# Four batches of value-head sums, gate products on VectorE, and an exchanged pair of loads in a fused attention-plus-MLP block

## The chip, the cores and the metric

One core of one Trainium2 chip. The time is the device time of one execution in microseconds (us). Most executions of one kernel agree within about 0.3%. All runs told here are with a granted clock of 0.999 or 1.0.

Engines in the profile: PE is TensorE's matmuls, PEld its weight loads, DVE is VectorE, ACT ScalarE, POOL GpSimd, SP SyncE. `L1374` is line 1374 of the kernel that ran; the changed kernel's lines are moved against those of before (its L723 is L720 of before, L1374 is L1335, L1220 is L1204, L1274 is L1253; with the bank edit of the experiments L1374 becomes L1376).

## The reference, cut to what matters

```python
# S = 2048 tokens, D = 640, H = 32 heads of 20, window W = 8 with dilation 2, F = 1536; bf16
xn = layernorm(x)
q, k, v = split(xn @ wqkv)                       # [H, S, 20] each
kg, vg = k[s - 2*w], v[s - 2*w]                  # w = 0..7, masked where s - 2*w < 0
attn = softmax(sum_d(q * kg) * scale)            # [H, S, 8]
o = sum_w(attn * vg)                             # the "value head sums"
h = (xn @ w_gate) * (xn @ w_up)                  # the gate product, no activation
out = x + o @ wo + h @ w_down
```

## The kernel before

A small scheduler inside the kernel orders the work of all engines at build time: each piece is a `Task` on an engine, and the scheduler orders instructions from its own estimate of when each will end.

The loads at the start. All but one small transfer (`touch`, by ScalarE) go out through SyncE, one after the other; `x_load` is a tile of 128 tokens (160 KB), `wqkv_load(0, 0, 3)` the first three fifths of the Q columns (480 KB), here "the Q rows".

```python
x_load(0, land=3.2)
...
wqkv_load(0, 0, 3, land=5.3)
x_load(1, land=5.7)
wqkv_load(0, 3, NCH, land=7.0)
```

The value sums. VectorE multiplies probabilities with values (`PV`), GpSimd adds pairs (`SV`), and TensorE sums over the window with a 128x32 selector. A unit is one chunk of one block of 512 tokens, 20 units in all. `BATCH` names the last unit of each batch of sums on TensorE, and each unit takes one bank.

```python
NU = NJ * NCH
BATCH = (1, 4, 6, 9, 11, 14, 19)
...
for u, b in zip(us, bs):
    for dq in range(4):
        ... e.matmul(PS[32*dq:32*dq+32, b, :], SEL[:], SV[sv_of[u]][:, dq, :], ...)
```

The gate product: gate and up projection of 128 features each fill a bank; ScalarE copies gate to SBUF, then either VectorE multiplies it with the up bank, or ScalarE copies that too and GpSimd multiplies.

```python
def mul():
    X = op("dve", lambda e: e.tensor_tensor(h, h, PS[:, hold[1], :], ALU.mult), ...)
    K.free_bank(hold[1], X)
...
if on_pool(j, m):
    ...  # ScalarE copies the up bank into us, GpSimd multiplies h by us
```

The choice of a bank: of the free banks, the one that is free earliest by the scheduler's estimate.

```python
def choose(self, k, free):
    if not k.contig:
        return [b for _, b in free[:k.banks]]
...
def free_bank(self, b, X):
    self.banks[b] = X.end + 0.05
```

Of the kernel before, what the change touches and what calls it, by code (L numbers as in the profile page):

```python
# [6 lines left out]
ALU = mybir.AluOpType  # L7
# [3 lines left out]
D = 640  # L11
# [4 lines left out]
NF = 12  # L16
# [5 lines left out]
TS = 128  # L22
JB = 512
# [332 lines left out]
def build_kernel(nc, A_x, A_wqkv, A_wo, B_x, B_w_gate, B_w_up, B_w_down, out):  # L356
# [41 lines left out]
    SV += [sb("SV3", [128, 4, JB], at=a_qk + 33024), sb("SV4", [128, 4, JB], at=a_qk + 33024 + 4096)]  # L398
    SV += [sb("SV5", [128, 4, JB], at=a_ra + 6 * D * 2)]
    sv_free = [3, 4, 0, 1, 2]  # L400
    a_sc = place[0]
# [10 lines left out]
    LOG = [sb(f"LOG{i}", [128, 2, W, TS]) for i in range(2)]  # L412
    HX = [sb(f"HX{i}", [128, JB], at=place[0] - 8192 + i * 1024) for i in range(8)]
    PRD += [sb("PRD9", [128, 4, JB], at=place[0])]
    HX += [sb(f"HX{8 + i}", [128, JB]) for i in range(4)]
    ATX0 = sb("ATX0", [128, 2, 2, JB])
# [13 lines left out]
    NUX = 3  # L430
    UX = sb("UX", [128, NUX, JB])
    STATS = sb("STATS", [128, NT, 12], FP32)
    MV = sb("MV", [128, NT, 2], FP32)
    SD = sb("SD", [128, NT, 4], FP32)
    DUM = sb("DUM", [128, 16], FP32)
    TCH = sb("TCH", [128, NCH, 32])
    ZERO = sb("ZERO", [128, JB])
    EPSC = sb("EPSC", [128, 16], FP32)
    IDENT = sb("IDENT", [128, 128])
# [5 lines left out]
    def ht(j, m):  # L445
        if j == 3:
            return XNT[:, m % NCH, m // NCH * JB:(m // NCH + 1) * JB]
        if j == 2:
            return OT[:, 3, m - 8, :] if m >= 8 else HX[HXM[m]][:]
        return HT[:, j, m, :]  # L450

    HXM = (0, 1, 2, 3, 8, 9, 10, 11, 4, 5, 6, 7)
    WPOS = (2, 0, 1)
# [6 lines left out]
    def bump(*k):  # L460
        count[k] = count.get(k, 0) + 1
# [45 lines left out]
    def wqkv_load(g, lo=0, hi=NCH, eng="sp", land=None):  # L507
        dst = WQKV[:, WPOS[g], lo:hi, :]
        dma(dst, wqkv_src[:, lo:hi, g * D:(g + 1) * D], w=[dst], name=f"ld_wqkv{g}_{lo}", eng=eng, land=land)
# [324 lines left out]
    def products():  # L834
        rows = {j: [] for j in range(NJ)}
        holds = {}
        for at, (j, kind) in enumerate(ORDER):
# [10 lines left out]
            if len(rows[j]) == 10 - 3 * len(QUAD.get(j, ())):  # L848
                K.spawn(logits(j, rows[j]))
        mark("products")  # L850
# [109 lines left out]

    def logits(j, slots):
        hold = []
        for e in slots:
            if len(e) > 3:
                yield lambda: len(e[3]) == 2
        slots.sort(key=lambda e: -e[2])
        n1 = sum(e[2] for e in slots)

        def go(*bs):
            for i, e in enumerate(slots):  # L970
                n, s, r = e[:3]
                b, i, nt = bs[1 - r], i - (0 if r else n1), n1 if r else len(slots) - n1
                for a in range(4):
                    o = PS[32 * a:32 * a + 32, b, :].rearrange("p (q s) -> p q s", q=4)
                    x = s[:, :, a * TS:(a + 1) * TS]
                    op("pe", (lambda o, x, i, a, nt: lambda e: e.matmul(o, G[:], x, start=(i == 0), stop=(i == nt - 1),  # L976
                                                                   tile_position=(0, 32 * a)))(o, x, i, a, nt),
                       r=[G[:], x], w=[o], name=f"lg{j}_{r}_{i}_{a}", occ=0.054, lat=0.4, mode=1)
                free.append(n)
            hold.extend(bs)  # L980

        def dst(r):
            return LOG[j // 2][:, j % 2, 4 * r:4 * r + 4, :]

        def ev(r):
            b, d = hold[1 - r], dst(r)
            X = op("act", lambda e: e.activation(d, PS[:, b, :].rearrange("p (q s) -> p q s", q=4), ACT.Copy, scale=SCALE),  # L987
# [8 lines left out]

        yield Task("pe", go, r=[e[1][:] for e in slots], prio=9.5, banks=2, slack=2.0 if j in QUAD else 0.5)
        bump("lg")
        for r in (1, 0):
            yield Task("act", lambda: ev(r), r=[PS[:, hold[1 - r], :]], w=[dst(r)], prio=2)  # L1000
        bump("logits", j // 2)

# [62 lines left out]
    NU = NJ * NCH  # L1065
    BATCH = (1, 4, 6, 9, 11, 14, 19)

# [43 lines left out]
    def unit(u):  # L1111
# [3 lines left out]
        yield have("vx", u)  # L1115
        if not more and count.get(("dn", 0), 0) >= 8:
            more.append(1)
            sv_free.extend(range(NS, len(SV)))
        yield lambda: len(sv_free) > 0 and (sv_free[0] in (3, 4) or count.get(("lg",), 0) >= NJ)
# [100 lines left out]

    ucount = [0]

    def on_pool(j, m):
        return count.get(("lg",), 0) >= NJ and m < 11 and ucount[0] - count.get(("hp",), 0) < HP_MAX

    def gu(j):
# [14 lines left out]
        for m in range(NF):  # L1241
# [15 lines left out]
            def after(h=h, hold=hold, j=j, m=m):  # L1257
# [11 lines left out]
                if on_pool(j, m):  # L1269
# [18 lines left out]
                    return  # L1288
                yield Task("dve", mul, r=[h, PS[:, hold[1], :]], prio=H_PRIO)

# [28 lines left out]
    def dn_piece(j, t, nb, rows, c0, c1):  # L1319
# [64 lines left out]
        K.spawn(tail())  # L1384

    SLIP = 0.3
    N_PE_T = 4
# [6 lines left out]
    GU_KEEP = 3  # L1394
    HP_MAX = 2
    ORDER = ((0, "n"), (1, "n"), (2, "n"), (3, "n"), (2, "w"), (3, "w"))
    LAST = ORDER[-1][0]
    HP_PRIO = 30
    DN_KEEP = 3
    H_PRIO = 9  # L1400
# [4 lines left out]
    stores.append(dma(TCH[0:16], tch, w=[TCH[0:16]], name="touch", eng="act"))  # L1405
    wqkv_load(0, 0, 3, land=5.3)
    x_load(1, land=5.7)
    wqkv_load(0, 3, NCH, land=7.0)
# [70 lines left out]
```

## Time and profile before

| | before |
|---|---|
| time, 3 runs | 267.78 us median (267.72 to 267.81) |
| span of the profiled execution | 266.0 us |
| TensorE busy | 98% |
| batches of value sums on TensorE | 7 |
| first 25 projection matmuls start | 6.39 us |
| row of 50 projection matmuls starts | 8.69 us |
| from there to the last addition on VectorE | 254.98 us |

The last line leaves out the first 9 us (loads from memory) and the last 2.3 us (stores to memory). I call it "the body".

### The profile page before, as it was taken

Reading aid. Unit: us, or ns where it says so; the run is one execution under the profiler, and the core shown is the slowest. Engines: PE = TensorE matmul, PEld = TensorE weight load, DVE = VectorE, ACT = ScalarE, POOL = GpSimd, SP = SyncE. Lnnn points to the kernel's source line nnn. Section 1 sums busy time; section 2 is a strip of 40 time slices with the busy share of each in tenths; the row PEclk is TensorE's granted clock in tenths of the full one; section 3 lists DMA queues with packets and bytes.
Section 4 is the critical chain, followed back from the end, with each engine's and each line's share of the span. In section 5 each row is a group of like instructions: output and inputs, shape, how many; then the busy total and the mean of one; then the engine's idle time right before and its main releaser. Section 6 shows DMA issues by size and latency. Waiting matters only on the chain.

```text
span 266.0 us, 4403 instructions
## 1 busy us (share of the span) xinstructions
PE 260.7 (98%) x1747; PEld 151.8 (57%) x1764; DVE 217.0 (82%) x249; ACT 112.0 (42%) x203; POOL 154.5 (58%) x99
## 2 busy tenths in 40 slices
PE   8999999999999999999999999999999999999996
PEld 5996965444444444444444444667466746774775
DVE  4687899999998699898699998998699979961211
ACT  3469997556622212242365426432443243116100
POOL 3000000000644996299955599999999989999000
DMA  7963689960489993831399143553885385006101
GB/s 211 372 208 78 126 149 382 385 248 1 124 147 192 241 212 75 166 76 30 73 334 201 36 112 83 133 147 80 182 181 157 85 146 112 2 0 94 32 25 53
DMA packets 39685, 37.84 MB, mean 142 GB/s; under 512 B 15824, under 2 KB 37328, under 8 KB 39632
## 3 DMA queue, kind: packets, MB, share of 16 engines
q1 hardware_dynamic: 36688, 31.35, 43.6%
q0 software_dynamic: 2736, 6.16, 13.6%
q8 instruction: 14, 0.23, 0.4%
q10 hardware_dynamic: 240, 0.05, 0.1%
q14 instruction: 7, 0.06, 0.1%
HBM read 25.07 MB, written 7.23 MB: 121 GB/s over the span
## 4 chain that ended last, share of the span: by engine, by line
PE 92%; ACT 5%; issue 1%; DVE 0%
PE PS L1253 39%; PE PS L1335 28%; PE PS L688 17%; ACT XNS L599 3%; PE PS L976 2%; PE PS L720 2%; PE PS L1204 2%; PE PS L672 2%; ACT QT L693 1%; ACT VST L693 1%; PE PS L632 1%; ACT KT L693 1%; ACT SD L574 0%; ACT HX L693 0%; DVE XNT L642 0%
## 5 line engine op out<-in xcount | busy, mean ns | idle before, releaser
L1154 POOL TENSOR_TENSOR SV<-PV 128x1024 bf16<-128x1024 f32 x40 | 95.0, 2535 | 9.6 <-DVE LOG L1033 3.3
L1149 DVE TENSOR_TENSOR PV<-VX,PS 128x1024 f32<-128x1024 bf16 (+1 forms) x54 | 91.0, 1729 | 5.4 <-POOL SV L1154 4.5
L688 PE MATMUL PS<-XNT,WQKV 128*128 128x512 bf16 (+2 forms) x384 | 60.0, 315 | 0.7 <-issue 0.5
L1253 PE MATMUL PS<-XNT,WG 128*128 128x512 bf16 x235 | 58.6, 379 | 0.3
L1253 PE MATMUL PS<-XNT,WU 128*128 128x512 bf16 x234 | 58.4, 379 | 0.4 <-ACT HX L693 0.2
L688 PEld LDWEIGHTS PS<-XNT,WQKV 128*128 128x128 bf16 x390 | 37.8, 112 | 22.1 <-ACT LOG L987 0.8
L1253 PEld LDWEIGHTS PS<-XNT,WU 128*128 128x128 bf16 x240 | 23.2, 98 | 29.0 <-issue 0.8
L1253 PEld LDWEIGHTS PS<-XNT,WG 128*128 128x128 bf16 x240 | 23.5, 98 | 27.8
L910 DVE TENSOR_TENSOR PRF<-PS,KT 128x1024 f32<-128x1024 f32 x32 | 37.8, 1216 | 0.3 <-PE PS L688 0.3
L693 ACT ACTIVATE HT<-PS 128x512 bf16<-128x512 f32 x24 | 14.3, 597 | 41.9 <-PE PS L1253 41.9
L936 POOL TENSOR_TENSOR PRF<-PRF,PRF 128x1024 f32<-128x1024 f32 x8 | 18.8, 2359 | 21.8 <-DVE LOG L1033 20.6
L1335 PE MATMUL PS<-WD,HT 128*128 128x320 bf16 x192 | 28.7, 299 | 0.0
L693 ACT ACTIVATE FB<-PS 128x320 bf16<-128x320 f32 x24 | 10.5, 438 | 41.1 <-PE PS L1335 38.4
L863 DVE TENSOR_TENSOR PRD<-QT,KT 128x2048 bf16<-128x2048 bf16 x24 | 27.3, 1217 | 0.0
L1335 PE MATMUL PS<-WO,OT 128*128 128x320 bf16 (+1 forms) x165 | 27.0, 295 | 0.0
L995 POOL MEMSET LOG<- 32x6 bf16 (+6 forms) x7 | 0.4, 95 | 44.2 <-ACT LOG L987 44.2
L1335 PEld LDWEIGHTS PS<-WD,HT 128*128 128x128 bf16 x192 | 18.6, 98 | 8.2 <-ACT FB L693 0.4
L1262 DVE TENSOR_TENSOR HT<-HT,PS 128x512 bf16<-128x512 bf16 x24 | 16.4, 685 | 8.0 <-PE PS L1253 7.9
L1335 PEld LDWEIGHTS PS<-WO,OT 128*128 128x128 bf16 x165 | 15.8, 98 | 6.2 <-issue 0.4
L954 POOL TENSOR_TENSOR PRD<-PRF,PRF 128x1024 bf16<-128x1024 f32 x8 | 18.7, 2354 | 0.9 <-DVE PRF L910 0.8
L1348 DVE TENSOR_TENSOR FB<-PS,XR 128x320 bf16<-128x320 f32 (+1 forms) x9 | 4.1, 454 | 15.3 <-PE PS L1335 15.3
L564 DVE BATCH_NORM_STATS2 STATS<-XST 128x6 f32<-128x320 bf16 x32 | 14.1, 471 | 2.4 <-DMA XST<-in_A_x_dram 2.4
(69 smaller groups left out, 238.9 us busy)
## 6 DMA issues: line engine op xcount, KB each, us to landing
VX<-v_scratch SPq DMA_DIRECT2D x80, 130.0 KB, 3.0
PRF<-PRF POOLq DMA_DIRECT2D x8, 512.0 KB, 5.2
XST<-in_A_x_dram SPq DMA_DIRECT2D x16, 160.0 KB, 5.6
v_scratch<-VST SPq DMA_DIRECT2D x4, 640.0 KB, 5.8
WG<-in_B_w_gate_dram SPq DMA_DIRECT2D x1, 1920.0 KB, 7.9
WU<-in_B_w_up_dram SPq DMA_DIRECT2D x1, 1920.0 KB, 11.9
out_dram<-in_A_x_dram SPq DMA_DIRECT2D x1, 1920.0 KB, 18.4
WD<-in_B_w_down_dram SPq DMA_DIRECT2D x1, 1920.0 KB, 8.5
```

The lines of the kernel that those rows point to most:

```text
L564: op("dve", lambda e: e.bn_stats(o, a), r=[a], w=[("st", t, i)], name=f"bn{t}_{i}", occ=0.49)
L688: op("pe", (lambda o, l, x, c, first: lambda e: e.matmul(o, l, x, start=first, stop=(c == NCH - 1)))(o, l, x, c, first), r=[l, x], w=[o], ...
L693: X = op("act", (lambda o, i: lambda e: e.activation(o, i, ACT.Copy))(o, i), r=[i], w=[o], name=name, occ=0.12 + n * 0.9e-3)
L863: op("dve", lambda e: e.tensor_tensor(s[:], qb, kv, ALU.mult), r=[q, rk], w=[s[:]], name=f"prod{j}_{r}_{c}", occ=1.15, lock=True)
L910: X = op("dve", lambda e: e.tensor_tensor(o[:], qb, kv, ALU.mult), r=[q, rk, ("qev", j, c)], w=[o[:]], name=f"prow{j}_{r}_{c}_{q0}", occ=1.17)
L936: yield Task("pool", lambda: op("pool", lambda e: e.tensor_tensor(x, x, y, ALU.add), r=[x, y] + tokens(), w=[x], name=name, occ=2.36, lock ...
L954: yield Task("pool", lambda: op("pool", lambda e: e.tensor_tensor(o, a, y, ALU.add), r=[a, y] + tokens(), w=[o], name=f"qend{j}_{r}_{q0}", ...
L1149: op("dve", lambda e: e.tensor_tensor(p, vw, a, ALU.mult), r=[vv] + rk, w=[p], name=f"pv{u}_{x}_{r0}", occ=0.09 + 1.1 * nr)
L1154: X = op("pool", lambda e: e.tensor_tensor(o, p[:, :, 0, :], p[:, :, 1, :], ALU.add), r=[p[:]] + tokens(), w=[o], name=f"pva{u}_{x}", occ= ...
L1253: op("pe", (lambda l, x, c: lambda e: e.matmul(PS[:, b, :], l, x, start=(c == 0), stop=(c == NCH - 1)))(l, x, c), r=[l, x], w=[PS[:, b, :] ...
L1262: X = op("dve", lambda e: e.tensor_tensor(h, h, PS[:, hold[1], :], ALU.mult), r=[h, PS[:, hold[1], :]], w=[h], name=f"h{m}_{j}", occ=0.65)
L1335: op("pe", (lambda l, x, i: lambda e: e.matmul(dst, l, x, start=(i == 0), stop=(i == n - 1)))(l, x, i), r=[l, x], w=[PS[:, b, :]], name=f" ...
```

## The change

The intent: three switches of TensorE between 128-wide and 32-wide matmuls fewer; gate products taken off GpSimd so that GpSimd's additions are ready for the larger batches; and the second token tile loaded ahead of the Q rows, so that VectorE need not wait for it. Cut to its core (more `SV` buffers, the three steps in which they come free, and a way to join logits that is switched off are left out):

```diff
-    BATCH = (1, 4, 6, 9, 11, 14, 19)
+    BATCH = (4, 9, 14, 19)
...
-                yield Task("dve", mul, r=[h, PS[:, hold[1], :]], prio=H_PRIO)
+                if not fast(j, m):
+                    yield Task("dve", mul, r=[h, PS[:, hold[1], :]], prio=H_PRIO)
+                    return
+                k0 = fcount[0]
+                fcount[0] += 1
+                us = UF[k0 % NUF][:]
+
+                def fev():
+                    K.free_bank(hold[1], evac([(us, PS[:, hold[1], :], JB)], f"uev{m}_{j}"))
+
+                def fmul():
+                    op("dve", lambda e: e.tensor_tensor(h, h, us, ALU.mult), r=[h, us], w=[h], name=f"h{m}_{j}", occ=0.34, lock=True)
...
+    FAST = [(2, m) for m in range(NF)]
...
-    HP_MAX = 2
+    HP_MAX = 0
...
-    DN_KEEP = 3
+    DN_KEEP = 5
...
-    wqkv_load(0, 0, 3, land=5.3)
-    x_load(1, land=5.7)
+    x_load(1, land=3.65)
+    wqkv_load(0, 0, 3, land=5.75)
```

`HP_MAX = 0` ends the gate products on GpSimd. `FAST` names those of the third block, whose up bank ScalarE copies to SBUF. The fourth block's are multiplied straight from PSUM by VectorE. `DN_KEEP` is how many free banks a piece of the down projection must leave: five, so that a batch of five finds its banks.

More of the change, by code (lines that the diff above doesn't have):

```diff
@@ L399, in build_kernel @@
     SV += [sb("SV5", [128, 4, JB], at=a_ra + 6 * D * 2)]
+    SV += [sb(f"SV{6 + i}", [128, 4, JB], at=a_ra + NF * JB * 2 + i * 4096) for i in range(3)]
     sv_free = [3, 4, 0, 1, 2]
@@ L412, in build_kernel @@
     LOG = [sb(f"LOG{i}", [128, 2, W, TS]) for i in range(2)]
-    HX = [sb(f"HX{i}", [128, JB], at=place[0] - 8192 + i * 1024) for i in range(8)]
+    HX = [sb(f"HX{i}", [128, JB], at=place[0] - 8192 + i * 1024) for i in range(4)]
+    SV += [sb("SV9", [128, 4, JB], at=place[0] - 4096)]
     PRD += [sb("PRD9", [128, 4, JB], at=place[0])]
-    HX += [sb(f"HX{8 + i}", [128, JB]) for i in range(4)]
+    HX += [sb(f"HX{4 + i}", [128, JB]) for i in range(4)]
     ATX0 = sb("ATX0", [128, 2, 2, JB])
@@ L431, in build_kernel @@
     UX = sb("UX", [128, NUX, JB])
+    NUF = 2
     STATS = sb("STATS", [128, NT, 12], FP32)
@@ L437, in build_kernel @@
     ZERO = sb("ZERO", [128, JB])
+    UF = [sb("UF0", [128, JB], at=a_xr + 4 * D * 2), ZERO]
     EPSC = sb("EPSC", [128, 16], FP32)
@@ L448, in ht @@
         if j == 2:
-            return OT[:, 3, m - 8, :] if m >= 8 else HX[HXM[m]][:]
+            return OT[:, 3, m - 8, :] if m >= 8 else HX[m][:]
         return HT[:, j, m, :]
-    HXM = (0, 1, 2, 3, 8, 9, 10, 11, 4, 5, 6, 7)
     WPOS = (2, 0, 1)
@@ L835, in products @@
         rows = {j: [] for j in range(NJ)}
+        joined = []
         holds = {}
@@ L848, in products @@
             if len(rows[j]) == 10 - 3 * len(QUAD.get(j, ())):
-                K.spawn(logits(j, rows[j]))
+                if j in JOIN:
+                    joined.append((j, rows[j]))
+                    if len(joined) == len(JOIN):
+                        K.spawn(logits(*joined))
+                else:
+                    K.spawn(logits((j, rows[j])))
         mark("products")
@@ L959, in close, with logits @@
         parts.append(q0)
-    def logits(j, slots):
+    def logits(*blocks):
         hold = []
-        for e in slots:
-            if len(e) > 3:
-                yield lambda: len(e[3]) == 2
-        slots.sort(key=lambda e: -e[2])
-        n1 = sum(e[2] for e in slots)
-        def go(*bs):
-            for i, e in enumerate(slots):
-                n, s, r = e[:3]
-                b, i, nt = bs[1 - r], i - (0 if r else n1), n1 if r else len(slots) - n1
-                for a in range(4):
-                    o = PS[32 * a:32 * a + 32, b, :].rearrange("p (q s) -> p q s", q=4)
-                    x = s[:, :, a * TS:(a + 1) * TS]
-                    op("pe", (lambda o, x, i, a, nt: lambda e: e.matmul(o, G[:], x, start=(i == 0), stop=(i == nt - 1),
-                                                                   tile_position=(0, 32 * a)))(o, x, i, a, nt),
-                       r=[G[:], x], w=[o], name=f"lg{j}_{r}_{i}_{a}", occ=0.054, lat=0.4, mode=1)
-                free.append(n)
+        for _, slots in blocks:
+            for e in slots:
+                if len(e) > 3:
+                    yield (lambda p: lambda: len(p) == 2)(e[3])
+            slots.sort(key=lambda e: -e[2])
+        def go(*bs):
+            for k, (j, slots) in enumerate(blocks):
+                n1 = sum(e[2] for e in slots)
+                for i, e in enumerate(slots):
+                    n, s, r = e[:3]
+                    b, i, nt = bs[2 * k + 1 - r], i - (0 if r else n1), n1 if r else len(slots) - n1
+                    for a in range(4):
+                        o = PS[32 * a:32 * a + 32, b, :].rearrange("p (q s) -> p q s", q=4)
+                        x = s[:, :, a * TS:(a + 1) * TS]
+                        op("pe", (lambda o, x, i, a, nt: lambda e: e.matmul(o, G[:], x, start=(i == 0), stop=(i == nt - 1),
+                                                                           tile_position=(0, 32 * a)))(o, x, i, a, nt),
+                           r=[G[:], x], w=[o], name=f"lg{j}_{r}_{i}_{a}", occ=0.054, lat=0.4, mode=1)
+                    free.append(n)
@@ L980, in go, with dst, ev @@
             hold.extend(bs)
-        def dst(r):
+        def dst(j, r):
             return LOG[j // 2][:, j % 2, 4 * r:4 * r + 4, :]
-        def ev(r):
-            b, d = hold[1 - r], dst(r)
+        def ev(k, j, r):
+            b, d = hold[2 * k + 1 - r], dst(j, r)
             X = op("act", lambda e: e.activation(d, PS[:, b, :].rearrange("p (q s) -> p q s", q=4), ACT.Copy, scale=SCALE),
@@ L995, in ev @@
                         op("pool", (lambda m: lambda e: e.memset(m, NEG))(m), w=[m], name=f"mask{w}", occ=0.2)
-        yield Task("pe", go, r=[e[1][:] for e in slots], prio=9.5, banks=2, slack=2.0 if j in QUAD else 0.5)
-        bump("lg")
-        for r in (1, 0):
-            yield Task("act", lambda: ev(r), r=[PS[:, hold[1 - r], :]], w=[dst(r)], prio=2)
-        bump("logits", j // 2)
+        yield Task("pe", go, r=[e[1][:] for _, slots in blocks for e in slots], prio=9.5, banks=2 * len(blocks),
+                   slack=2.0 if blocks[-1][0] in QUAD else 0.5)
+        for _ in blocks:
+            bump("lg")
+        for k, (j, _) in enumerate(blocks):
+            for r in (1, 0):
+                yield Task("act", (lambda k, j, r: lambda: ev(k, j, r))(k, j, r), r=[PS[:, hold[2 * k + 1 - r], :]], w=[dst(j, r)], prio=2)
+            bump("logits", j // 2)
     def softmax(x):
@@ L1115, in unit @@
         yield have("vx", u)
-        if not more and count.get(("dn", 0), 0) >= 8:
-            more.append(1)
-            sv_free.extend(range(NS, len(SV)))
+        for k, (ok, n) in enumerate(((("atx", 1) in done, (9,)), (count.get(("dn", 0), 0) >= 8, (5,)),
+                                     (count.get(("dn", 1), 0) >= 8, (6, 7, 8)))):
+            if ok and k not in more:
+                more.append(k)
+                sv_free.extend(n)
         yield lambda: len(sv_free) > 0 and (sv_free[0] in (3, 4) or count.get(("lg",), 0) >= NJ)
@@ L1221, in build_kernel, with fast @@
     ucount = [0]
+    fcount = [0]
+    def fast(j, m):
+        return (j, m) in FAST
     def on_pool(j, m):
@@ L1288, in after @@
                     return
-                yield Task("dve", mul, r=[h, PS[:, hold[1], :]], prio=H_PRIO)
+                if not fast(j, m):
[8 more added lines that the diff above has]
+                    op("dve", lambda e: e.tensor_tensor(h, h, us, ALU.mult), r=[h, us], w=[h], name=f"h{m}_{j}", occ=0.34, lock=True)
+                    bump("hf")
+                    bump("h", j)
+                yield num(k0 - NUF + 1, "hf")
+                yield Task("act", fev, r=[PS[:, hold[1], :]], w=[us], prio=7)
+                yield num(k0, "hf")
+                yield Task("dve", fmul, r=[h, us], prio=H_PRIO, lock=True)
             yield Task("pe", lambda b: go(0, b), prio=50, banks=1, keep=GU_KEEP, r=[WG[:]])
@@ L1384, in dn_piece @@
         K.spawn(tail())
+    FAST = [(2, m) for m in range(NF)]
+    JOIN = ()
     SLIP = 0.3
```

## The prediction

> **What bounds the kernel now.** I read the page first (engine totals, the chain that ended last), then the timeline of each engine, then the order of the instructions of both kernels.
>
> The page, engine totals and chain by engine:
>
> ```profile
> PE 260.7 (98%) x1747; PEld 151.8 (57%) x1764; DVE 217.0 (82%) x249; ACT 112.0 (42%) x203; POOL 154.5 (58%) x99
> PE 92%; ACT 5%; issue 1%; DVE 0%
> ```
>
> TensorE is busy in 98% of the span and is 92% of the chain. Busy matmuls overlap, so I checked it by pitch. From the timeline a 512-column matmul starts every 0.2158 us (five in 1.079), a 320-column one every 0.1358, a 128-column one every 0.0565, a 256-column one every 0.109. By the instruction order there are 200 + 480 of the first kind, 527 of the second, and after the first tile 155 of the third and 110 of the fourth: 146.7 + 71.6 + 8.8 + 12.0 = 239.1. The 112 logit and 80 value-sum matmuls in their 11 batches take 12.7 (0.0536 us each and 0.215 us a batch, worked out below), 15 transposes 0.9, the 34 half-wide ones at the end 2.4. That is 255.1, against 255.0 us between 8.69 and 263.67: from 8.69 us on, TensorE has no air that such a count could find. Only removed TensorE work, or an earlier start, can make the kernel faster; a new wait of TensorE makes it slower one for one.
>
> The chain shows ACT from 21 to 35 us. It isn't a bound: in that stretch matmuls also stand pitch to pitch (170 in 26.4 us, against 25.9 by count).
>
> The start, all engines' timeline (start, length, engine, line, in brackets the idle time before and what ended it):
>
> ```profile
> 5.77 0.89 DVE L564 BATCH_NORM_STATS2 STATS<-XST 128x6 f32<-128x320 bf16 x2 [0.26 <-DMA XST<-in_A_x_dram]
> 6.38 1.44 PEld L720 LDWEIGHTS PS<-XNT,WQKV 128*128 128x128 bf16 x25 [0.24 <-ACT XNT L644]
> 7.46 0.64 DVE L593 TENSOR_SCALAR XNS<-XST,MV,SD 128x384 bf16<-128x384 bf16 x2
> 7.89 0.37 PEld L632 LDWEIGHTS PS<-IDENT,XNS 128*128 128x128 bf16 x5
> 8.28 0.36 DVE L642 COPY XNT<-PS 128x384 bf16<-128x384 bf16 x1 [0.18 <-PE PS L632]
> 8.69 2.83 PEld L720 LDWEIGHTS PS<-XNT,WQKV 128*128 128x128 bf16 x50 [0.42 <-DVE XNT L642]
> ```
>
> VectorE waits 0.26 us for the second token tile. But the transposes of that tile (7.89) come right behind the 25 matmuls of the first tile, whose issue ends at 6.38 + 1.44 = 7.82.
>
> A value-sum batch on TensorE, between gate and up groups:
>
> ```profile
> 164.91 1.24 PE L1253 MATMUL PS<-XNT,WG 128*128 128x512 bf16 x5
> 166.08 0.83 PE L1204 MATMUL PS<-SV,SEL 128*32 128x512 bf16 x12
> 166.84 1.25 PE L1253 MATMUL PS<-XNT,WU 128*128 128x512 bf16 x5
> ```
>
> GpSimd while the first five units' products are added, with its gate products (L1279) between:
>
> ```profile
> 137.71 4.68 POOL L1154 TENSOR_TENSOR SV<-PV 128x1024 bf16<-128x1024 f32 x2 [3.08 <-DVE LOG L1019]
> 142.34 1.17 POOL L1279 TENSOR_TENSOR HX<-HX,UX 128x512 bf16<-128x512 bf16 x1
> 146.67 2.36 POOL L1154 TENSOR_TENSOR SV<-PV 128x1024 bf16<-128x1024 f32 x1 [3.16 <-DVE SM L1006]
> 148.98 1.16 POOL L1279 TENSOR_TENSOR HX<-HX,UX 128x512 bf16<-128x512 bf16 x1
> 153.40 4.67 POOL L1154 TENSOR_TENSOR SV<-PV 128x1024 bf16<-128x1024 f32 x2 [3.25 <-DVE LOG L1033]
> 160.25 4.67 POOL L1154 TENSOR_TENSOR SV<-PV 128x1024 bf16<-128x1024 f32 x2
> ```
>
> The tenth add, which completes unit 4, ends at 164.92; its sums start at 166.08.
>
> **What the Trainium skill says.** (1) "TensorEngine Tiling (Array Packing)", section Key Properties: changing the tiling mode drains TensorE. The trace agrees: the 128x32 batch above starts 0.09 us later than the pitch allows (164.91 + 1.079 = 165.99), and see below. (2) "SBUF — State Buffer", section Who interferes with whom: a VectorE instruction with two SBUF inputs contends with a GpSimd instruction that reads SBUF, exclusively. No run yet shows the blocking; the program orders the two by semaphores, and the 3.1 us gaps of GpSimd ended by VectorE are that order. (3) "VectorE: DVE Perf Modes", section The perf-mode tier table: a two-tensor product of bf16 in SBUF runs two elements a cycle, with an operand in PSUM one. The trace agrees: 512 columns take 685 ns with a PSUM operand (L1262) and 424 ns all in SBUF (the bf16 maximum of L1006).
>
> **The change, part by part.**
>
> *Batches of value sums, seven to four.* From the last matmul's pitch to the first normal matmul, a batch of 8 takes 0.65 us (141.59 to 142.24), of 12 0.85 (165.99 to 166.84), of 20 1.29 (243.66 to 244.95). So 0.0536 us a matmul and 0.215 us a batch. The matmuls stay 80. Three batches fewer: 3 x 0.215 = 0.65 us less, all on TensorE, so all of it on the end.
>
> *Second token tile first.* x1 now goes ahead of the first Q rows on the same queue. All the same bytes had landed by 5.77, when x1, then third, was there; so the Q rows land by about 5.8 at the latest, before 6.38, when the first matmul waits for ACT anyway. x1's statistics start when VectorE is done with tile 0 (5.51), 0.26 earlier. But the transposes can't start before 7.82: of 0.26 us, 0.07 us remain.
>
> *Gate products.* Ten GpSimd products go (10 x 1.16 = 11.6 us of GpSimd). The twelve of block 2 are copied to SBUF by ACT and multiplied on VectorE at 424 ns (before: eight at 685), those of block 3 all from PSUM at 685 (before: six). VectorE: 12 x 0.424 + 12 x 0.685 - 14 x 0.685 = +3.7 us. ACT: 12 copies more, 10 fewer, +1.2 us. None lies on TensorE. Block 2's banks now come free by ACT alone, so TensorE depends less on VectorE there. The ten more lock points between VectorE and GpSimd take the place of GpSimd's own products.
>
> *Five-wide batches and later starts of the down projection* need up to five of the six free banks. After a batch the next matmul needs a bank back: ACT frees the first about 1.1 us after the start, the batch lasts 1.2, as in the last batch of before. No new wait.
>
> *When each batch is needed.* By the instruction order the first batch of five stands one gate/up pair earlier than unit 4's sums did. Before had 31 groups of 1.079 us and a batch of 8 between 131.86 and 165.99; the changed kernel has 30 groups and no batch: 131.86 + 32.37 + 0.09 = 164.3, less the 0.07 of the start. For unit 4 I put the new order together from row durations (product 2.20 or 1.14 pitch, add 2.32, fast product 0.36, hand-over 0.06): subtraction done 138.65, adds ending at 141.07, 146.95, 151.34, 154.24, 157.14, 161.56 and 163.88. So unit 4 is ready some 0.3 us before it is needed, against 1.16 before. The later batches: ten more adds each (23.2 + 0.85 us of accumulate issue) give about 188, 212 and 236, against needs at about 190.6, 216.8 and 239.9.
>
> *Sum:* -0.65 - 0.07 = -0.72 us if no wait appears: 267.06. With an even error of some 0.7 us in my 0.3 us margin, I charge 0.1 us: 267.1 us, 0.25% faster.
>
> **Rivals.**
>
> *The first batch waits for GpSimd.* For: the margin of 0.3 us, and each of the twelve fast products holds the adds behind a hand-over. Against: GpSimd loses four products (4.6 us) before that point. A wait of 0.5 to 1.2 us eats the gain: 267.5 to 268.3.
>
> *VectorE or GpSimd becomes the bound late.* VectorE has 67.0 us of value products from unit 5 to 19, nine products of block 3 (5.4) and some 2 us of waits for ACT: about 160 + 75 = 235, then GpSimd's last adds by 237 to 239, against 239.9. If the two engines lock-step worse than that, the last batch stalls TensorE by one to two us: 268 to 269.
>
> *The start gains its whole 0.26 us* if the transposes were held by the tile and not by the queue of matmuls: 266.9. Against: 7.82 and 7.89 in the timeline. Or the Q rows land late and the first matmul waits, which would cost a few tenths.
>
> **Range and chances.** No wait at all is 267.0 to 267.1, with 0.3 either way for the batch cost and the start; a stall of up to a microsecond is about one chance in four. So 267.1, from 266.5 to 268.2. Faster by 2% needs 262.4: 5.4 us, and TensorE has no such air; 0.01. Slower by 2% needs 273.1, a stall of 6 us: 0.02. Within 2%: 0.97.
>
> **What would show it.** Right: four rows of value sums of 20 matmuls, each with 0.215 us of switch; TensorE pitch to pitch elsewhere; the second 50-matmul row starting at about 8.6; GpSimd without gate products, its tenth add ending near 163.9; fast products at 424 ns. Wrong: idle time of TensorE ended by GpSimd before the first or last batch; value products waiting so long for adds that GpSimd's last add passes 240; a first matmul held by the Q rows' load; or a gain over 1.1 us, which would mean that TensorE had air that I did not see.

## The result, and the profile after

| | before | after |
|---|---|---|
| time, 4 runs each of the same rounds | 267.76 us (267.72 to 267.81) | 268.19 us (267.75 to 268.27) |
| span of the profiled execution | 266.0 us | 266.5 us |
| row of 50 starts | 8.69 us | 9.40 us |
| body | 254.98 us | 254.80 us |

The ratio is 1.0012, 95% interval 0.9995 to 1.003: the same, and by the median 0.4 us longer. A ratio is computed as the mean time of one kernel's fast runs over that of the other's of the same rounds, so it isn't quite the ratio of the medians quoted. The four runs of after are 268.24, 268.27, 268.14 and 267.75 us; the profiled one is the first.

The page of after, engine totals and the chain by engine:

```profile
PE 261.1 (98%) x1764; PEld 152.2 (57%) x1764; DVE 219.4 (82%) x259; ACT 113.0 (42%) x205; POOL 143.6 (54%) x89
PE 96%; DMA 2%; DVE 1%; SPq 0%; issue 0%
```

GpSimd has ten instructions fewer, VectorE ten more, as forecast. New in the chain is DMA with 2%, and VectorE has 1% instead of 0%: 2% of 266.5 us is 5.3 us at the start.

**Where the time came back: the batches.** Of the timeline of TensorE after, the last batch:

```profile
239.87 1.24 PE L1274 MATMUL PS<-XNT,WG 128*128 128x512 bf16 x5
241.04 1.26 PE L1220 MATMUL PS<-SV,SEL 128*32 128x512 bf16 x20
242.24 1.25 PE L1274 MATMUL PS<-XNT,WU 128*128 128x512 bf16 x5
```

239.87 + 5 x 0.2158 is 240.95: the batch starts 0.09 us late. From its start to the next normal matmul are 1.20 us, of which 20 x 0.0536 = 1.07 are matmuls: 0.13 us on the way out. That is the 0.215 us a batch of the prediction. Four such rows stand in the trace instead of seven.

**Where it went, first: the start.** The chain of after, its first pieces (start, length, what):

```profile
1.72 5.27 DMA WQKV<-in_A_wqkv_dram
...
7.13 1.65 PE PS L723 x25
...
9.40 2.99 PE PS L723 x50
```

The Q rows are issued at 1.72 us, behind x1, and are complete at 7.00. The first 25 projection matmuls start at 7.13 instead of 6.39, and the row of 50 at 9.40 instead of 8.69: 0.71 us. The timeline of after says that nothing else held them:

```profile
5.36 0.88 DVE L567 BATCH_NORM_STATS2 STATS<-XST 128x6 f32<-128x320 bf16 x2
5.72 0.77 ACT L647 ACTIVATE XNT<-PS 128x384 bf16<-128x384 bf16 x2 [1.14 <-PE PS L635]
7.13 1.65 PE L723 MATMUL PS<-XNT,WQKV 128*128 128x128 bf16 x25 [1.00 <-DMA WQKV<-in_A_wqkv_dram]
```

The second tile's statistics (first line) have lost their wait for DMA, as intended. ScalarE has the first tile's transposes ready at 6.49, the first half of them at 6.22, which is enough for the first matmuls (see e4_before_swap). TensorE stands idle for 1.00 us in front of its first projection until the load ends.

Why so late? The table by stretch of time, of before, for two stretches of 0.6 us (columns: the stretch, its length, busy time of each engine, the granted clock, the DMA engines' busy share and GB/s):

```profile
2.80:3.40 0.60, 0.60 (x5) 0.40 (x4) 0.23 (x1) 0.00 (x0) 0.44 (x3) 1.00 0.64 132
3.40:4.00 0.60, 0.60 (x4) 0.42 (x3) 0.60 (x2) 0.00 (x0) 0.36 (x3) 1.00 0.99 346
```

And of after, the same two stretches:

```profile
2.80:3.40 0.60, 0.60 (x5) 0.41 (x4) 0.28 (x1) 0.00 (x0) 0.43 (x3) 1.00 0.91 237
3.40:4.00 0.60, 0.60 (x4) 0.43 (x3) 0.60 (x2) 0.00 (x0) 0.36 (x3) 1.00 0.52 96
```

There is a lull in the transfers just before the Q rows begin to flow. Before, it lies at 2.8 to 3.4 us (132 GB/s), after at 3.4 to 4.0 us (96 GB/s): the Q rows' stream starts later by about one such stretch. In the three stretches behind the lull it runs at 346 to 388 GB/s before and at 305 to 365 GB/s after. On top of this comes spread. The trace has the moment at which each of a load's 16 parts ended. Before, those of the Q rows ended between 4.72 and 5.28 us, with the median at 4.82; after, between 5.13 and 7.00, with the median at 5.51. The last part of all decides: the 15th ended at 6.26. Why the parts spread more is not shown. The Trainium skill states, in "DMA: Bandwidth & Descriptors", section Two DMAs through the same engine are not ordered, that nothing orders transfers across the 16 engines. The trace agrees: the Q rows' last part ended at 7.00 us, 0.74 us behind their 15th, and the next load of SyncE had its first part in at 5.97.

**Where it went, second: a bank.** The timeline of TensorE, ScalarE and VectorE around the first batch of after:

```profile
163.88 1.24 PE L1274 MATMUL PS<-XNT,WU 128*128 128x512 bf16 x5
...
165.06 1.26 PE L1220 MATMUL PS<-SV,SEL 128*32 128x512 bf16 x20
165.53 2.56 ACT L1229 ACTIVATE OT<-PS 128x512 bf16<-128x512 f32 x5 [0.85 <-PE PS L1220]
165.99 0.68 DVE L1283 TENSOR_TENSOR XNT<-XNT,PS 128x512 bf16<-128x512 bf16 x1
...
166.73 1.94 PE L1374 MATMUL PS<-WD,HT 128*128 128x320 bf16 x13 [0.41 <-DVE XNT L1283]
```

The batch holds five banks, and the down projection behind it needs one. It got the bank of an up projection whose gate product on VectorE runs from 165.99 to 166.67. So it starts 1.67 us after the batch instead of 1.20, and 0.48 us are lost. ScalarE frees the batch's own first bank at about 165.53 + 2.56 / 5 = 166.04, earlier; but the scheduler had, by its estimate, taken VectorE's for the earlier one. The waits of TensorE after, beside the one for the zeroed tile at the very start, say the same in three lines:

```profile
PE PS L723 <- DMA WQKV<-in_A_wqkv_dram: 1.0, 1, 1.0
PE PS L1374 <- DVE XNT L1283: 0.4, 1, 0.4
PE PS L723 <- DVE XNT L645: 0.3, 1, 0.3
```

The third stands in before too. **The sum:** start +0.71, bank +0.48, three batches -0.65: +0.54, against a span that grew by 0.5 us.

**GpSimd and VectorE.** From the timelines of after, the additions that end units 4 and 19 (counted from 0; the last of the first and of the fourth batch) and one fast product:

```profile
159.81 4.67 POOL L1170 TENSOR_TENSOR SV<-PV 128x1024 bf16<-128x1024 f32 x2 [2.00 <-DVE PV L1165]
164.52 0.43 DVE L1321 TENSOR_TENSOR OT<-OT,ZERO 128x512 bf16<-128x512 bf16 x1 [0.20 <-POOL SV L1170]
...
234.71 4.67 POOL L1170 TENSOR_TENSOR SV<-PV 128x1024 bf16<-128x1024 f32 x2 [0.16 <-DVE PV L1165]
```

The tenth addition ends at 164.48, its batch starts at 165.06; the last ends at 239.38, its batch starts at 241.04. TensorE waits for GpSimd nowhere.

### The profile page after: what moved, and what is told of

Read it like the earlier page. It is cut to its first block, busy times and chain, and to the rows that moved or that the text cites. A ratio compares the mean times of both kernels' runs of the same rounds, so it can differ in the third digit from the quotient of the medians.

```text
span 266.5 us, 4425 instructions
## 1 busy us (share of the span) xinstructions
PE 261.1 (98%) x1764; PEld 152.2 (57%) x1764; DVE 219.4 (82%) x259; ACT 113.0 (42%) x205; POOL 143.6 (54%) x89
## 4 chain that ended last, share of the span: by engine, by line
PE 96%; DMA 2%; DVE 1%; SPq 0%; issue 0%
PE PS L1274 39%; PE PS L1374 28%; PE PS L691 23%; PE PS L987 2%; PE PS L723 2%; DMA WQKV<-in_A_wqkv_dram 2%; PE PS L1220 2%; SPq L479 0%; PE PS L635 0%; DVE XNT L1283 0%; DVE XNT L645 0%; DVE FB L1387 0%
## 5 line engine op out<-in xcount | busy, mean ns | idle before, releaser
L691 PE MATMUL PS<-XNT,WQKV 128*128 128x512 bf16 (+2 forms) x390 | 60.9, 316 | 0.0
L1274 PE MATMUL PS<-XNT,WU 128*128 128x512 bf16 x240 | 59.7, 379 | 0.0
L1274 PE MATMUL PS<-XNT,WG 128*128 128x512 bf16 x240 | 59.6, 379 | 0.0
L1283 DVE TENSOR_TENSOR XNT<-XNT,PS 128x512 bf16<-128x512 bf16 x12 | 8.2, 684 | 9.4 <-PE PS L1274 9.3
```

The source lines that it names most:

```text
L691: op("pe", (lambda o, l, x, c, first: lambda e: e.matmul(o, l, x, start=first, stop=(c == NCH - 1)))(o, l, x, c, first), r=[l, x], w=[o], ...
L1274: op("pe", (lambda l, x, c: lambda e: e.matmul(PS[:, b, :], l, x, start=(c == 0), stop=(c == NCH - 1)))(l, x, c), r=[l, x], w=[PS[:, b, :] ...
```

## The experiments

Theory A: the two losses are the Q rows' late landing and the bank behind the first batch, and with both taken away the kernel gains the 0.65 us of the three batches. Rivals: the losses are of another kind (the gate products' move, the order of the batches), or the late landing was the chance of one execution.

In the table, "start" runs from the first statistics on VectorE to the row of 50, which takes out when the first tile landed; "Q rows" is the end of the last of the 16 parts. The kernel before ran beside each set.

| run | loads | first bank, second bank | time, us | ratio to before | Q rows, us | start, us | body, us |
|---|---|---|---|---|---|---|---|
| before, first profile | old | - | 267.76 | | 5.28 | 5.52 | 254.98 |
| after, first profile | new | VectorE, as built | 268.19 | 1.0012 | 7.00 | 6.28 | 254.80 |
| e0_after_again | new | as after | 267.67 | 1.0 | 6.30 | 5.40 | 254.81 |
| e1_load_order | old | as after | 267.76 | 0.9999 | 4.94 | 5.26 | 254.80 |
| e2_bank | new | ScalarE, VectorE | 267.56 | 0.999 | 6.53 | 5.57 | 254.44 |
| e3_both | old | ScalarE, VectorE | 267.19 | 0.9978 | 5.22 | 5.70 | 254.51 |
| e4_before_swap | new | before's program | 267.87 | 1.0006 | 6.34 | 5.58 | 254.98 |
| e8_actq | old, x1 by ScalarE | ScalarE, VectorE | 267.47 | 0.9995 | 5.40 | 5.64 | 254.42 |
| e10_banks2 | old | ScalarE, ScalarE | 267.34 | 0.9985 | 5.12 | 5.41 | 254.32 |
| e14_banks2_again | old | ScalarE, ScalarE | 267.02 | 0.997 | 5.20 | 5.26 | 254.32 |
| e11_two_first | two tiles first | ScalarE, ScalarE | 267.49 | 0.9983 | 7.49 | 6.65 | 254.32 |

e5_seven, e12_gates and e13_dvegates change the batches or the gate products and are told below. The kernel before had 267.85 us beside e0 to e3, 267.73 beside e4, e5, e8 and e10, and 267.74 beside the last four. Each experiment had five or six runs.

### Two causes, four combinations

**e0_after_again**: the changed kernel as it is.

> The changed kernel as it is, to have its spread beside the others. Theory (the start is late by the order of the loads, and one bank wait): 268.2 us, about 0.4 above before, the first projection matmul at 7.1 us and an idle 0.4 us of TensorE before the first down projection. Rival (chance: one slow DMA packet fell on the Q rows in the profiled run): the runs spread between 267.4 and 268.3, and the start of the first projection differs from run to run by as much as 0.7 us, also towards 6.4.

Measured: 267.67 us (267.29 to 268.29), ratio 1.0 (0.9987 to 1.0012). The body repeats to 0.01 us. The start doesn't repeat: 5.40 us instead of 6.28. The Q rows were late again, at 6.30 us, but the first matmul waited only 0.2 us for them. So the times spread as the rival said, while the landing was late a second time, as the theory said.

**e1_load_order**: the two loads as before, the rest as after.

```diff
-    x_load(1, land=3.65)
-    wqkv_load(0, 0, 3, land=5.75)
+    wqkv_load(0, 0, 3, land=5.3)
+    x_load(1, land=5.7)
```

> The changed kernel with the first two loads in the order of before (Q rows, then second token tile); all other engines keep the same instructions in the same order. Theory: the Q rows land at about 5.3 us again, the first projection matmul starts at 6.4, the second row of 50 at 8.7, and the time falls by 0.7 us to 267.5. Rival (chance): the time stays at 268.2 and the start varies as much as with the other order.

Measured: 267.76 us (267.30 to 268.08), ratio 0.9999. The Q rows are back at 4.94 us, and no matmul waits for them. The expected 267.5 us is missed: in time this pair shows no difference (267.76 against 267.67), and runs of one and the same kernel differ by up to a microsecond here.

**e2_bank**: as after, but the first down piece behind the first batch gets another bank. The edit tells the scheduler that the bank in question comes free a microsecond later; it then hands out the batch's first. The order of instructions on every engine stays that of after.

```diff
                     K.free_bank(hold[1], X)
+                    if (j, m) == (3, 2):
+                        K.banks[hold[1]] += 1.0
```

> The changed kernel with its own load order, but the first piece of the first down projection gets the bank of the first value sum (freed by ACT) instead of the bank freed by VectorE's third gate product of block 3; all orders are the same. Theory: the 0.4 us of idle TensorE before that piece are gone, the down projection starts 1.29 us after the end of the last up group, 0.48 us less: 267.7. Rival: another wait takes its place, ACT's copy of the first value sum or the third gate product's bank one piece later, and the time stays within 0.1 us of 268.2.

Measured: 267.56 us (267.0 to 267.88), ratio 0.999. The body fell from 254.80 to 254.44, by 0.36 and not by the whole 0.48 us.

**e3_both**: both edits.

> The load order of before and the other bank together. Theory: both costs are gone and only the three saved batches stay: 0.65 us below before, 267.1. If the two waits hide each other, less than the sum of the two single gains: 267.4 or so. If the batches saved nothing: 267.7, as before.

Measured: 267.19 us (267.01 to 267.43), ratio 0.9978 (0.9966 to 0.999): faster than before by 0.22%. The body, 254.51 us, is 0.47 us below that of before, so a part of the 0.66 us between the medians is chance or the start. Where the missing tenth went, the timeline of e3 shows, at the first and the second batch:

```profile
165.74 2.29 PEld L1376 LDWEIGHTS PS<-WD,HT 128*128 128x128 bf16 x18 [0.42 <-ACT OT L1229]
```

```profile
190.79 1.26 PE L1220 MATMUL PS<-SV,SEL 128*32 128x512 bf16 x20
192.08 3.43 PE L1376 MATMUL PS<-WD,HT 128*128 128x320 bf16 x24
```

Behind the first batch nothing is lost any more: the down piece starts 1.19 us after the batch's start (164.55), with a bank that ScalarE's copy freed. Behind the second are 1.29 us instead of 1.20: everything had moved forward by 0.48 us, and here too the down piece had a bank that VectorE frees, which had been free in time only because TensorE was late.

### Is that the whole of the bank's part?

**e10_banks2**, and again as **e14_banks2_again**: the same edit for the second batch as well.

```diff
-                    if (j, m) == (3, 2):
+                    if (j, m) in ((3, 2), (3, 5)):
```

> Old load order, and both first down pieces behind the first and the second batch of value sums get a bank that ScalarE frees (the run before mended only the first). Theory: TensorE has no wait for VectorE behind either batch; from the first down piece of the second batch on it is 0.1 us earlier, the stretch from the row of 50 to the end is 254.35 to 254.45 us against 254.5; time 267.0 to 267.15, 0.25 to 0.3 per cent below the kernel before. Rival (the 0.1 us turns up again in a later wait, as a part of the first bank's gain did): stretch 254.5, time as with one bank mended, 267.2.

> The run with both banks mended once more, as the anchor of this set: stretch from the row of 50 to the last addition 254.3 us, time 267.0 to 267.4, below the kernel before by 0.1 to 0.25 per cent.

Measured: bodies 254.32 us in both; times 267.34 (267.06 to 267.84) and 267.02 (266.83 to 267.33); ratios 0.9985 (0.9972 to 0.9997) and 0.997 (0.9957 to 0.9982). The first time misses what was expected (267.0 to 267.15), its profiled execution (267.06) doesn't; the second, 0.3% below the kernel before, is a little better than expected. The second batch of e10:

```profile
190.50 1.26 PE L1220 MATMUL PS<-SV,SEL 128*32 128x512 bf16 x20
191.70 2.48 PE L1376 MATMUL PS<-WD,HT 128*128 128x320 bf16 x17
```

1.20 us, without a wait. The body is 254.98 - 254.32 = 0.66 us below that of before: the three batches, to 0.01 us. After's body is this plus 0.48 us, that of e2 this plus 0.1. So the account of the body closes to 0.02 us. This version, with the old order of the loads, is the best, 0.15 and 0.3% below the kernel before.

### Is a batch really worth 0.215 us?

**e5_seven**: e3 with the seven batches of before, and so the moved gate products alone.

```diff
-    BATCH = (4, 9, 14, 19)
+    BATCH = (1, 4, 6, 9, 11, 14, 19)
```

> The run with the old load order and the mended bank, but with the value sums in the seven old batches. Theory (a batch costs 0.215 us of switching on TensorE, so three cost 0.65): the stretch from the row of 50 to the end is 0.65 us longer than with four batches, less the 0.1 us that a bank wait still took behind the second batch of 20: 255.05 to 255.2 against 254.5; time 0.5 to 0.65 us above the four-batch run, so about that of the kernel before, which means that the move of the gate products buys no time by itself. Rival (batches cost only what the down projection waits make of them): stretch and time within 0.2 us of the four-batch run.

Measured: body 254.99 us, 267.84 us (267.75 to 268.02), ratio 1.0005. Against e10 the body is 0.67 us longer, against e3 (which still had the second bank's 0.1) 0.48; the expected 255.05 to 255.2 us were a little too much. It is the body of before to 0.01 us. So the moved gate products by themselves buy nothing, and the batches 0.65 us; the rival, that the batches only matter by their banks, falls.

### The loads

**e4_before_swap**: the kernel before with the two loads exchanged and nothing else.

```diff
-    wqkv_load(0, 0, 3, land=5.3)
-    x_load(1, land=5.7)
+    x_load(1, land=3.65)
+    wqkv_load(0, 0, 3, land=5.75)
```

> The kernel before with the two loads exchanged and nothing else (order of instructions as before). Theory (the Q rows land later and the first matmul waits for them): the Q rows' last piece lands between 6.3 and 7.0 us instead of 5.0 to 5.3, TensorE waits 0.1 to 0.7 us for DMA in front of its first 25 projection matmuls, the row of 50 starts 5.6 to 6.3 us after the first statistics instead of 5.5; everything after that row as in the kernel before (254.98 us from the row of 50 to the last addition on VectorE). Time 0.1 to 0.6 us above the kernel before. Rival (my prediction: all bytes are there by 5.8 either way): Q rows by 5.8, first matmul waits for ACT, row of 50 starts 0.07 us earlier, time 0.07 us below the kernel before.

Measured: 267.87 us (267.8 to 268.09), ratio 1.0006 (0.9992 to 1.0019). The Q rows end at 6.34, a microsecond later than with the old order, and TensorE's first row starts late by it, although the view names ScalarE as what ended the idle time:

```profile
5.67 0.76 ACT L644 ACTIVATE XNT<-PS 128x384 bf16<-128x384 bf16 x2 [1.05 <-PE PS L632]
6.45 1.52 PEld L720 LDWEIGHTS PS<-XNT,WQKV 128*128 128x128 bf16 x25 [0.57 <-ACT XNT L644]
```

The row waits for the load and for ScalarE, and the view names only one of them. With the old order, here in e1, ScalarE's two copies stand at the same time, and the row starts before the second has ended:

```profile
5.66 0.77 ACT L647 ACTIVATE XNT<-PS 128x384 bf16<-128x384 bf16 x2 [1.05 <-PE PS L635]
6.21 1.44 PEld L723 LDWEIGHTS PS<-XNT,WQKV 128*128 128x128 bf16 x25 [0.33 <-ACT XNT L647]
```

So the first copy is enough. In all nine profiles in which SyncE issues the Q rows right behind the first tile, the row's first weight load starts 0.04 us after that copy has signalled its end; in all five in which they stand behind x1, it starts 0.10 us after the last part of the Q rows. By this comparison the landing held TensorE in each of the five: by 0.84 us in after, 0.10 in e0, 0.15 in e2, 0.24 here and 1.35 in e11. The late landing and its cost came as the theory expected. The time, 0.14 us above before by the medians, is inside the noise and can't confirm a cost of this size. The body is that of before. My own forecast of a gain of 0.07 us isn't to be seen (the start took 5.58 us, against 5.52 in the profile of before).

**e11_two_first**: e10 with two token tiles ahead of the Q rows, the suspected cost doubled, with every engine's order of work unchanged.

```diff
-    wqkv_load(0, 0, 3, land=5.3)
     x_load(1, land=5.7)
+    x_load(2, land=9.0)
+    wqkv_load(0, 0, 3, land=5.3)
     wqkv_load(0, 3, NCH, land=7.0)
     wqkv_load(1, 0, 3, land=8.5)
-    x_load(2, land=9.0)
```

> As the anchor, but with two token tiles (x1 and x2) issued ahead of the Q rows instead of none: the suspected cost doubled; every engine's order of work as in the anchor. Theory (the Q rows' landing moves with what is issued ahead of them, and once it is past the 6.3 to 6.5 us at which the first matmul could start, every tenth of a us of it is on the end): Q rows land at 7.0 to 7.7, TensorE waits 0.6 to 1.3 us for DMA, the row of 50 starts 6.2 to 6.9 us after the first statistics instead of 5.4 to 5.6, the stretch behind it stays 254.3, time 0.6 to 1.3 us above the anchor. Rival (the late load of the changed kernel's profile was one straggling transfer engine and the order matters little): row of 50 within 5.4 to 5.7, time within 0.2 us of the anchor.

Measured: in the profiled execution the Q rows end at 7.49 us (median of their parts 6.04), and the first matmul waits for them. The timeline of it:

```profile
7.62 1.60 PE L723 MATMUL PS<-XNT,WQKV 128*128 128x128 bf16 x25 [1.44 <-DMA WQKV<-in_A_wqkv_dram]
```

The start takes 6.65 us instead of 5.26 in e14 of the same set: 1.4 us. The time: 267.49 us (267.18 to 268.32) against 267.02, so 0.47 us by the medians. The profiled execution was the slowest of the five (268.32), the fastest was only 0.35 us above the fastest of e14. So the direction holds, the landing varies between executions, and the profile of one shows only that one. By the medians the expectation of 0.6 to 1.3 us was too high. The lull moved once more: by the same table of stretches it lies at 4.0 to 4.6 us (124 GB/s).

**e8_actq**: e3 with x1 issued by ScalarE, so that the Q rows keep their early place at SyncE.

```diff
+    x_load(1, "act", land=5.7)
     tch = A_wqkv.rearrange("(c k p) n -> k c p n", k=16, c=NCH)[:, :, 0, 0:32]
...
-    x_load(1, land=5.7)
```

> Mended bank, Q rows issued first by SyncE at about 1.27 us, x1 issued at about the same time by ScalarE. If the lateness of the Q rows comes from their place behind x1 in one engine's issues: the Q rows land by 5.3 and x1 near 4, first matmul waits for ACT, row of 50 starts 0 to 0.07 us earlier than with the old order; time 0 to 0.1 us below the run with the old order and the mended bank. If it comes from the 164 KB ahead of or among them in the transfer engines: Q rows land at 6.0 to 7.0 whichever engine issues, TensorE waits 0 to 0.7 us for DMA, time 0.1 to 0.6 us above that run.

Measured: x1 ends at 3.81 us and the Q rows at 5.40, no matmul waits for either; so x1's bytes, which here too came in ahead of them, are not what makes the Q rows late, and the place behind x1 at the one issuing engine is the likelier cause. But in this profile the very first tile ended at 3.60 us instead of 3.08 to 3.33 in the others, and the start took 5.64 us: no gain. The time, 267.47 us (267.31 to 268.33), ratio 0.9995 (0.9982 to 1.0009), tells it neither from e3 nor from before. The Trainium skill says in "DMA: Bandwidth & Descriptors", section Issuing engines are not separate DMA queues, that transfers run on the same 16 engines and interleave whoever issued them, and that several issuers save only the sequencer's time. Two numbers fit it: SyncE takes 0.39 to 0.49 us an issue, and the first tile got slower when ScalarE's transfer came beside it. One run is not a proof of that second reading.

### What the gate products' move is for

**e12_gates**: e10, four batches, gate products shared as before.

```diff
-    FAST = [(2, m) for m in range(NF)]
+    FAST = []
...
-    HP_MAX = 0
+    HP_MAX = 2
```

> As the anchor, with four batches, but with the gate products shared out as in the kernel before (some on GpSimd, none all in SBUF); the scheduler then puts the first batch three gate/up pairs later. Theory (the move of the gate products only serves to have the units ready in time): units become ready later; where the order leaves room TensorE has no wait and the stretch is 254.3 again; where not, TensorE waits for GpSimd in front of a batch, the first or the last, 0.3 to 2 us, and the stretch is 254.6 to 256.3. Rival (the move itself shortens TensorE's work, by banks that come free sooner): the stretch is longer without any wait of TensorE for GpSimd.

Measured: 267.71 us (267.34 to 267.78), ratio 0.999 (0.9977 to 1.0002); body 254.50 us, 0.18 more than e10. In front of the batches TensorE doesn't wait for GpSimd: the scheduler, which sees the units come later, puts the later batches later (the last at 243.50 us in its span). It waits behind the last one, for a gate product that GpSimd still had to do:

```profile
243.16 3.02 POOL L1302 TENSOR_TENSOR XNT<-XNT,UX 128x512 bf16<-128x512 bf16 x2
246.23 1.75 PEld L1376 LDWEIGHTS PS<-WD,XNT 128*128 128x128 bf16 x14 [0.34 <-POOL XNT L1302]
```

The product ends at 246.18. The matmul before this row started at 245.93, so the row is 0.17 us behind its pitch, and that is the 0.18 us but for 0.01. The wait for GpSimd came, then, but for a gate product and not, as I had expected, in front of a batch; the rival, a longer stretch without any wait for GpSimd, falls.

**e13_dvegates**: e10 with the third block's products straight from PSUM on VectorE.

```diff
-    FAST = [(2, m) for m in range(NF)]
+    FAST = []
```

> As the anchor, with four batches and no gate product on GpSimd, but block 2's twelve products straight from PSUM on VectorE (685 ns) instead of from copies in SBUF (424 ns): VectorE has 12 x 0.26 = 3.1 us more, ScalarE twelve copies less. The scheduler puts the first batch two pairs later. In the changed kernel the last add ended 1.6 us before its batch, so theory: up to 1.5 us of wait of TensorE for GpSimd in front of the last batch, or none if the order moved the batch enough: stretch 254.3 to 256. A bank wait behind the first batch (its first down piece has a bank that VectorE frees again) may add up to 0.5. Rival (VectorE's share has no part in the end): 254.3.

Measured: 268.49 us (268.47 to 268.66), ratio 1.0026 (1.0014 to 1.0039); body 255.65 us, 1.33 more than e10. The size was as expected, the place was not: TensorE doesn't wait in front of the last batch, but behind it. Its timeline there:

```profile
244.97 1.26 PE L1220 MATMUL PS<-SV,SEL 128*32 128x512 bf16 x20
...
246.17 0.71 PE L1376 MATMUL PS<-WO,OT 128*128 128x320 bf16 x2
247.06 0.31 PE L1376 MATMUL PS<-WO,OT 128*128 128x320 bf16 x1 [0.18 <-ACT OT L1229]
...
248.04 0.31 PE L1376 MATMUL PS<-WO,OT 128*128 128x320 bf16 x1 [0.18 <-ACT OT L1229]
```

With the batch so late, no other matmuls stand between it and the out projection, which takes the five sums one by one as ScalarE copies them, 0.49 us each instead of 0.1358 for a matmul. From 246.17 to the next row, at 248.18, five matmuls take 2.01 us instead of 5 x 0.1358 = 0.68: 1.33 us, the whole difference. So the fast products matter: they let the last batch stand at 241 us, with other matmuls between it and its use. Worth 1.3 us against this variant, and 0.2 against the share-out of before.

## Why the prediction was right or wrong

The class and the range held (268.19 in 266.5 to 268.2, at its very edge). The centre, 267.1, and the sign did not. That the range held is luck: its upper part was meant for a wait for GpSimd, which didn't come, and two other losses, of 0.71 and 0.48 us, happened to end inside it.

- **TensorE has no air: right.** The body moved with each tenth of a microsecond that TensorE won or lost.
- **Three batches are worth 0.65 us: right.** By e5, e10 and e14 0.66 to 0.67 us.
- **"All the same bytes had landed by 5.77 ... so the Q rows land by about 5.8 at the latest": wrong.** The step took the start for one continuous stream of bytes, whose order doesn't matter for its end. But the Q rows' stream starts behind a lull that moves with their issue (0.6 us later), and their 16 parts spread over more time. They landed at 6.30 to 7.00 us in all four profiles with the new order, against 4.94 to 5.73 in all nine with the Q rows issued first. The rival that I named in half a sentence, that they land late and the first matmul waits, came true in the profile of after, with 0.71 us. The other three with this order paid less, 0.10 to 0.24 us at the first matmul: ScalarE was ready for it at 6.2 to 6.5 us, and the landing must come 0.1 us earlier still to cost nothing. As the start of after's other executions isn't in any trace, it stays open whether the whole 0.4 us of the first set's medians is this; the body gained 0.18 us, so some 0.6 us would have to come from outside it, and the profiled execution has them at the start.
- **0.07 us from x1 ahead: not seen.** Its 0.26 us of VectorE's wait went, as forecast, and the transposes were held by TensorE's queue, as forecast. The late landing stood in its way in each profile of the new order, and starts with an equal order differ by more (5.26 us in e14, 5.88 in e12).
- **"No new wait" for a bank: wrong.** I had checked when ScalarE frees the first bank (my 1.1 us; measured about 1.0), but not which bank the next instruction is tied to. It was one of VectorE's: 0.48 us, the whole of it on the end; e2 and e10 show it by taking it away.
- **The margins of GpSimd: right.** In e10, whose start wasn't late, unit 4's sums were ready at 159.01 + 4.66 = 163.67 us (forecast 163.88) and the batch started at 164.25 (forecast 164.3): room of 0.58 us instead of 0.3, and the same 0.58 us in after, where both are later. The 0.1 us charged for a wait wasn't needed. The late bound of VectorE or GpSimd didn't come: last addition at 239.4, batch at 241.04.
- **The durations: right.** The fast product took 0.42 to 0.43 us; the Trainium skill's tier table, cited in the prediction, agrees with it.

In all: forecast -0.72 + 0.1 for a possible wait; measured in the profile -0.65 for the batches, +0.71 for the start, +0.48 for the bank.

## What to carry to other kernels

When a gain is a few tenths of a microsecond on an engine that has no air, check for each instruction behind the changed place which buffer it is tied to and who frees that one, not just whether some buffer is free; a static allocator that goes by estimates can pick the wrong one, and mending one such wait can uncover the next. The time at which a load must be complete is set by its last part, so put a load that the first matmul needs first at its issuing engine, and judge a change of its order by many executions and not by one profile. Where an instruction waits for two things, the view names one; a run in which the other is out of the way tells which of them held it. An engine that is off the critical path may still decide how early a batch can stand, and so whether there is other work to cover what follows it.

## What the Trainium skill lacked or had wrong

- "DMA: Bandwidth & Descriptors" says that nothing orders transfers across the 16 engines, but gives no size: the 16 parts of one 480 KB load ended within 0.56 us of each other in the profile of before and within 1.87 us in that of after.
- The same page says that the time to initiate a transfer is usually small relative to the transfer itself. By share that holds here (0.42 us of issue, 4.01 us from the issue of the Q rows to their last part in before). What it doesn't say is that one more issue ahead can cost more than its own time: with one more 160 KB load ahead at SyncE, the median part of the Q rows ended 0.69 us later and the last 1.72 us later.
- "TensorEngine Tiling (Array Packing)", section Key Properties, says that a change of mode drains TensorE, without a number: here 0.09 us into a 128x32 batch and 0.13 us out of it.
- No page that I read warns that the bank which a build-time scheduler hands out may be freed late by VectorE while ScalarE frees another sooner: 0.48 us at the first batch, and 0.1 us at the second once the first was mended.
